# A recurrent attention block with a feed-forward block behind it: chunks of 32 problems on four quarters of the array, two scans for the decay, and a written-out order for all engines

## The chip, the cores and the metric

The kernel runs on one core of one Trainium2 chip. A core has five engines that work at the same time and wait for each other by semaphores: TensorE (PE, matrix products from SBUF into PSUM; its weight loads are listed apart as PEld), VectorE (DVE), ScalarE (ACT), GpSimd (POOL) and SyncE (SP), which here only issues DMAs. Each engine takes its instructions in program order. The metric is the device time in microseconds, so less is better. All data are 32-bit floats.

## The reference

For each of 4 batches and 8 heads there is one recurrence over 768 tokens with a 40x40 state; these 32 (batch, head) pairs are the "problems".

```python
for t in range(S):
    y[:, :, t] = np.einsum('bhd,bhde->bhe', rt, state)
    Sa = np.einsum('bhde,bhe->bhd', state, at)
    state_decay = state * wt[:, :, None, :] - np.einsum('bhd,bhe->bhde', Sa, bt)
    state = state_decay + np.einsum('bhd,bhe->bhde', vt, kt)
```

The output, turned to 3072 tokens by 320 channels, is then the input of a feed-forward block:

```python
h = x @ w_in                        # 320 -> 2048
g = h * (1.0 / (1.0 + np.exp(-h)))  # SiLU
return (g @ w_out).astype(np.float32)   # 2048 -> 320
```

The two weight matrices arrive as 64-bit floats; the kernel turns them into 32-bit floats on the chip by integer operations on their two words.

## The kernel before

Tokens are cut into 12 chunks of 64. A chunk has two units (`m` = 0, 1) of two batches, 16 problems each. Within a chunk the recurrence becomes matrix work. With W the running product of the decay w, a is multiplied by W, and b and k are divided by it (`scale`: a scan on VectorE at line 209, a reciprocal at 218, products on GpSimd at 219 and 221). `between` (line 189) makes the 64x64 products of b and a, and of k and a, between the tokens of the chunk, masked on VectorE at 197. One plus the masked b-a matrix has to be inverted: `inverse` does this for the two 32x32 halves of the matrices of two chunks at once (64 problem-chunks, 128 matrices, one on each partition) by 31 rows of a multiply (258) and a sum (264) on VectorE. The matrices go to it through DRAM (`md`, line 241) and come back through `xd` and `zd` (272 to 290). `merge` (302, 319) joins the halves with 32x32 products.

`chain` is the part that depends on the state: `keys` turns k and b (365), `right` makes the right-hand sides (374, 386), `solve` applies the inverse (408, 426), `update` makes the next state (446 on TensorE, 461 and 464 on VectorE, 470 on GpSimd), `turn` transposes it (477), `read` and `write` make the output (488, 496, 508, 515, 526). The output goes by 16 DMAs a chunk (line 532) from `yx` to `xt`, with channels on partitions. The feed-forward part `moe` takes `xt`: 16 groups of three products (549, rows 120, 120 and 80), a sigmoid on ScalarE (557) and a product on VectorE (558), then 2 x 16 products of the second layer (566), a copy (575) and the DMAs out (578). `weights` (lines 134 to 147) converts 44 pieces of the weight matrices.

What sets the order: the program text. `weave` mixes lists of steps evenly: the steps of the chains of chunk n, those that prepare chunk n+2 (and every second chunk the rows of the inverse), and what waits of the feed-forward part. Inputs are loaded on SP's queue two chunks ahead, weights on ScalarE's queue. `sb.tile` with `bufs` gives several buffers in turn; PSUM has six banks for the recurrence (`bank`) and two for the feed-forward part (`moe_bank`). If a running product leaves its range, a slow exact version behind `tc.If` runs instead; with these inputs it doesn't.

Of the kernel before, what the change touches and what calls it, by code (L numbers as in the profile page):

```python
# [18 lines left out]

TT = C = 64
DP = 64
# [4 lines left out]
def weave(*lists):  # L33

    at = [(i + 0.5) / len(x) for x in lists for i in range(len(x))]
    steps = [s for x in lists for s in x]
    for i in sorted(range(len(steps)), key=lambda i: at[i]):
        steps[i]()
# [3 lines left out]
def kernel(  # L42
# [16 lines left out]
    NM, NN = aT.shape[0] // 2, aT.shape[1]  # L59
    B, S = v.shape[0], v.shape[1]  # L60
    D, H, P, Q = 40, 8, 4, 8
    DM, DF = w_in.shape[0], w_in.shape[1] // 2
    NF = DF // 128
    KT = (120, 120, 80)
    assert (B, NM, NN * C, DM) == (4, 2, S, 320)
# [7 lines left out]
    def bank(name):  # L73
        return ps.tile([128, 512], F32, name=name, tag="att", bufs=6)

    def moe_bank(name):
        return ps.tile([128, 512], F32, name=name, tag="moe", bufs=2)

    ident = const.tile([128, 128], F32, name="ident")
    make_identity(nc, ident)  # L80
    ms = sb.tile([128, 2, C], F32, name="ms")
    ml = sb.tile([128, C], F32, name="ml")
    for be in range(2):
        make_upper_triangular(nc, ml[C * be : C * be + C], diag=False)
    nc.vector.tensor_copy(out=ms[:, 0], in_=ml)
    nc.vector.tensor_scalar(out=ms[:, 1], in0=ml, scalar1=-1.0, scalar2=None, op0=ALU.mult)
    wi_s = const.tile([128, 3, DF], F32, name="wi_s")
    wo_s = const.tile([128, NF, DM], F32, name="wo_s")
    chk = const.tile([128, 2 * NM * NN], F32, name="chk")

    one = sb.tile([128, Q, C + 1], F32, name="one")
    hm = sb.tile([128, 2], F32, name="hm")
    low = sb.tile([128, 1], F32, name="low")
    nc.vector.memset(low, -896.0 * 2.0**23)
    G = [sb.tile([128, Q, D], F32, name=f"G{m}") for m in range(NM)]
    Gbd = [sb.tile([128, Q, 2, DP], F32, name=f"Gbd{m}") for m in range(NM)]
    GT = [sb.tile([128, Q, 128], F32, name=f"GT{m}") for m in range(NM)]
    RHS = [sb.tile([128, P, 2, DP], F32, name=f"RHS{m}") for m in range(NM)]
    XT = [sb.tile([128, NM, H, C], F32, name=f"XT{i}") for i in range(2)]
    XI = sb.tile([128, 32, 32], F32, name="XI")  # L100

    w0 = sb.tile([128, Q, C + 1], F32, name="w")
    early = [
        sb.tile([128, 32 * 32], F32, name=x)[:, 0 : Q * (C + 1)].rearrange("p (q t) -> p q t", q=Q)
        for x in ("tmp", "mi")
    ]
    for w in [w0] + early:
        nc.vector.memset(w, 1.0)
        nc.vector.memset(w[:, :, 0:1], 0.0)
    nc.vector.memset(one, 0.0)  # L110
    nc.vector.memset(one[:, :, 0:1], 1.0)
    nc.vector.memset(hm, 0.0)
    for j in range(2):
        nc.vector.memset(hm[DP * j : DP * j + DP, j : j + 1], 1.0)
    nc.vector.memset(XI, 0.0)
    nc.vector.memset(XI.rearrange("p s t -> p (s t)")[:, 0 : 32 * 32 : 33], 1.0)
    for t in G + Gbd + GT + RHS + XT:
        nc.gpsimd.memset(t, 0.0)
# [4 lines left out]
    WS = 256  # L123
    pieces = [(wi_s[0:n, k, c : c + WS], w_in[120 * k : 120 * k + n, 2 * c : 2 * (c + WS)])
              for c in range(0, DF, WS) for k, n in enumerate(KT)]
    wo_f = wo_s.rearrange("p c d -> p (c d)")
    for c in range(0, NF * DM, WS):
        pieces.append((wo_f[:, c : c + WS], w_out[:, 2 * c : 2 * (c + WS)]))

    def weights(n):  # L130
        dst, src = pieces[n]
        m = dst.shape[0]
        room = sb.tile([128, 4 * WS], I32, name=("tmp", "mi")[n % 2])[0:m]
        nc.scalar.dma_start(room[:, 0 : 2 * WS], src)
        words = room[:, 0 : 2 * WS].rearrange("p (c two) -> p c two", two=2)
        lo, hi = words[:, :, 0], words[:, :, 1]
        e, f = room[:, 2 * WS : 3 * WS], room[:, 3 * WS : 4 * WS]
        shr, band, bor = ALU.logical_shift_right, ALU.bitwise_and, ALU.bitwise_or
        nc.vector.tensor_scalar(out=e, in0=hi, scalar1=20, scalar2=0x7FF, op0=shr, op1=band)  # L139
        nc.vector.tensor_scalar(out=f, in0=hi, scalar1=0xFFFFF, scalar2=None, op0=band)  # L140
        nc.scalar.activation(out=e, in_=e, func=AF.Relu, scale=2.0**23, bias=low[0:m])
        nc.scalar.activation(out=f.bitcast(F32), in_=f, func=AF.Copy, scale=2.0**-20, bias=1.0)
        nc.scalar.activation(out=lo.bitcast(F32), in_=lo.bitcast(U32), func=AF.Copy, scale=2.0**-52)
        nc.vector.scalar_tensor_tensor(out=e, in0=hi, scalar=-(1 << 31), in1=e, op0=band, op1=bor)
        f, lo, e = (x.bitcast(F32) for x in (f, lo, e))
        nc.vector.tensor_tensor(out=f, in0=f, in1=lo, op=ALU.add)
        nc.vector.tensor_tensor(out=dst, in0=f, in1=e, op=ALU.mult)  # L147

    class Unit:
        pass  # L150

    def unit(n, m):
        u = Unit()
        u.n, u.m, u.i = n, m, NM * (n % 2) + m
        return u


    def load(u):
        u.a = sb.tile([128, Q, C], F32, name="a", bufs=4)
        u.kb = sb.tile([128, Q, 2, C], F32, name="kb", bufs=6)  # L160
        B2 = slice(2 * u.m, 2 * u.m + 2)
        for n, x in ((1, bT), (0, kT)):
            for be in range(2):
                nc.sync.dma_start(
                    u.kb[:, P * be : P * be + P, n], x[2 * u.m + be, u.n].rearrange("p (q t) -> p q t", q=P)
                )
        nc.sync.dma_start(
            u.a.rearrange("p (b q) t -> p b (q t)", b=2), aT[B2, u.n].rearrange("b p c -> p b c")
        )

    def load_w(u, at):
        u.w = at
        for be in range(2):
            for j in range(2):
                J = slice(DP * j, DP * j + D)
                nc.sync.dma_start(
                    at[J, P * be : P * be + P, 1 : C + 1],
                    wT[2 * u.m + be, u.n, J].rearrange("p (q t) -> p q t", q=P),
                )

    def between(u, n, s):

        pm = [bank("pm") for _ in range(2)]
        for p in range(P):
            for be in range(2):
                for j in range(2):
                    q = P * be + p
                    J = slice(DP * j, DP * j + DP)
                    nc.tensor.matmul(  # L189
                        pm[j][C * be : C * be + C, p * C : p * C + C],  # L190
                        lhsT=u.kb[J, q, n, :],
                        rhs=u.a[J, q, :],
# [13 lines left out]
    def pre(u, md):  # L206
# [24 lines left out]
        def scores():  # L231
# [3 lines left out]
            if u.m < NM - 1:  # L235
                return
# [559 lines left out]
```

## Time and profile before

| | |
|---|---|
| Three runs | 1112.42 us median, 1108.23 to 1114.07 |
| Profiled execution | span 1101.0 us, from its first to its last instruction; no other time of this execution is given |
| TensorE, weight loads | 865.9 us (79%), 701.6 us (64%), 11058 instructions each |
| VectorE, ScalarE, GpSimd | 620.7 us (56%), 314.1 us (29%), 126.2 us (11%) |
| Mean granted clock of TensorE | 0.931 of full speed |
| DMA | 80.68 MB in 205707 packets, 73 GB/s; 176656 packets under 512 B |

A row of the page's list of groups reads: line, engine, operation, output<-inputs, shape, count, then busy time and mean duration, then the idle time of the engine before these instructions and what ended it. The rows with ten digits per engine cut the span into 40 slices of 27.5 us; a 9 is 90% busy or more, and PEclk is the granted clock in tenths. One f32 product appears as two MATMUL instructions. Matmuls overlap each other, so a mean duration of one (250 ns for a small one) is much longer than the distance between two.

### The profile page before, as it was taken

Reading aid. Unit: us, or ns where it says so; the run is one execution under the profiler, and the core shown is the slowest. Engines: PE = TensorE matmul, PEld = TensorE weight load, DVE = VectorE, ACT = ScalarE, POOL = GpSimd, SP = SyncE. Lnnn points to the kernel's source line nnn. Section 1 sums busy time; section 2 is a strip of 40 time slices with the busy share of each in tenths; the row PEclk is TensorE's granted clock in tenths of the full one; section 3 lists DMA queues with packets and bytes.
Section 4 is the critical chain, followed back from the end, with each engine's and each line's share of the span. In section 5 each row is a group of like instructions: output and inputs, shape, how many; then the busy total and the mean of one; then the engine's idle time right before and its main releaser. Section 6 shows DMA issues by size and latency. Waiting matters only on the chain.

```text
span 1101.0 us, 25962 instructions
## 1 busy us (share of the span) xinstructions
PE 865.9 (79%) x11058; PEld 701.6 (64%) x11058; DVE 620.7 (56%) x1088; ACT 314.1 (29%) x736; POOL 126.2 (11%) x136
## 2 busy tenths in 40 slices
PE   0003746777969999699998699987999997999997
PEld 0002745654648786478776578775787775887875
DVE  7497468886961469913559805479515597131220
ACT  2003536543214321124421233311342211432120
POOL 6100102300001120001110002200011200000000
PEclk9999977789987899889999799998898998999999
DMA  5604443543023351034341215431324213020000
GB/s 135 134 15 115 125 115 101 141 113 87 11 66 86 95 121 37 13 80 112 82 120 25 56 31 128 97 88 29 74 71 101 74 36 77 10 73 17 7 19 15
DMA packets 205707, 80.68 MB, mean 73 GB/s; under 512 B 176656, under 2 KB 198160, under 8 KB 205584
## 3 DMA queue, kind: packets, MB, share of 16 engines
q1 hardware_dynamic: 199776, 68.46, 26.2%
q10 hardware_dynamic: 5808, 10.49, 3.3%
q8 instruction: 88, 1.44, 0.5%
q14 instruction: 35, 0.29, 0.1%
HBM read 61.60 MB, written 13.37 MB: 68 GB/s over the span
## 4 chain that ended last, share of the span: by engine, by line
PE 44%; DVE 31%; DMA 9%; SPq 7%; issue 4%; POOL 2%; ACT 2%; DVEq 0%; ACTq 0%; POOLq 0%
PE ph L549 13%; DVE tmp L258 10%; PE po L566 10%; DVE XI L264 7%; SPq L532 4%; DVE w L218 4%; PE pl L488 3%; DVE gts L558 2%; PE pm L189 2%; PE pr L386 2%; PE pq L302 2%; DVE W L209 2%; DMA tmp<-in_w_in 2%; DMA xt<-yx 2%; PE pg L446 2%
## 5 line engine op out<-in xcount | busy, mean ns | idle before, releaser
L549 PE MATMUL ph<-xt,wi_s 120*128 120x256 f32 (+1 forms) x1152 | 296.9, 410 | 69.2 <-DVE gts L558 56.0
L549 PEld LDWEIGHTS ph<-xt,wi_s 120*128 120x128 f32 (+1 forms) x1152 | 225.0, 203 | 123.7 <-DVE gts L558 72.1
L566 PE MATMUL po<-wo_s,gts 128*128 128x320 f32 x768 | 222.6, 445 | 13.6 <-DVE wo_s L147 7.7
L566 PEld LDWEIGHTS po<-wo_s,gts 128*128 128x128 f32 x768 | 146.0, 194 | 74.4 <-DVE wo_s L147 9.4
L558 DVE TENSOR_TENSOR gts<-ph,sg 128x256 f32<-128x256 f32 x192 | 79.6, 418 | 147.0 <-ACT sg L557 146.4
L258 DVE TENSOR_TENSOR tmp<-XI,mi 128x1 f32<-128x1 f32 (+30 forms) x186 | 139.8, 752 | 15.6 <-DMA mi<-md 11.1
L557 ACT ACTIVATE sg<-ph 128x256 f32<-128x256 f32 x192 | 73.3, 383 | 253.5 <-PE ph L549 244.8
L264 DVE TENSOR_REDUCE XI<-tmp 128x1 f32<-128x1 f32 (+30 forms) x186 | 93.3, 502 | 5.0
L221 POOL TENSOR_TENSOR kb<-kb,w 128x512 f32<-128x512 f32 x44 | 53.6, 1239 | 362.5 <-DVE w L218 277.8
L197 DVE TENSOR_TENSOR sk<-pm,ms 128x256 f32<-128x256 f32 x48 | 18.2, 419 | 134.6 <-PE pm L189 134.6
L302 PE MATMUL pq<-XT,sb 32*32 32x32 f32 x768 | 33.0, 206 | 74.7 <-DMA XT<-zd 74.7
L189 PE MATMUL pm<-a,kb 64*64 64x64 f32 x1536 | 48.5, 251 | 52.3 <-POOL kb L221 41.8
L302 PEld LDWEIGHTS pq<-XT,sb 32*32 32x32 f32 x768 | 30.8, 122 | 81.9 <-DVE mi L139 61.9
L189 PEld LDWEIGHTS pm<-a,kb 64*64 64x64 f32 x1536 | 39.0, 156 | 63.0 <-POOL kb L221 44.8
L218 DVE RECIPROCAL w<-W 128x512 f32<-128x512 f32 x22 | 73.7, 3348 | 0.8
L219 POOL TENSOR_TENSOR a<-a,W 128x512 f32<-128x512 f32 x24 | 28.9, 1204 | 346.3 <-DMA a<-in_aT 242.7
L526 DVE TENSOR_TENSOR yx<-py,W 64x512 f32<-64x512 f32 x48 | 33.0, 688 | 37.8 <-DMA xt<-yx 14.0
L480 ACT COPY GT<-pt 128x512 f32<-128x512 f32 x44 | 24.2, 586 | 85.9 <-PE pt L477 85.7
L488 PE MATMUL pl<-r,vut 64*128 64x64 f32 x768 | 46.5, 274 | 0.0
L488 PEld LDWEIGHTS pl<-r,vut 64*128 64x128 f32 x768 | 44.2, 188 | 3.4 <-issue 3.0
L575 ACT COPY ot<-po 128x320 f32<-128x320 f32 x24 | 10.2, 425 | 114.9 <-PE po L566 92.0
L470 POOL TENSOR_TENSOR G<-t,W 128x320 f32<-128x320 f32 x22 | 25.4, 1156 | 130.4 <-DVE t L461 130.4
(101 smaller groups left out, 966.3 us busy)
## 6 DMA issues: line engine op xcount, KB each, us to landing
kb<-in_bT SPq DMA_DIRECT2D x48, 128.0 KB
kb<-in_kT SPq DMA_DIRECT2D x48, 128.0 KB
a<-in_aT SPq DMA_DIRECT2D x24, 256.0 KB
vut<-in_vT SPq DMA_DIRECT2D x48, 128.0 KB
r<-in_rT SPq DMA_DIRECT2D x24, 256.0 KB
v<-in_v SPq DMA_DIRECT2D x48, 80.0 KB
vu<-in_v SPq DMA_DIRECT2D x24, 160.0 KB
xt<-yx SPq DMA_DIRECT2D x192, 20.0 KB
```

The source lines that it names most:

```text
L189: nc.tensor.matmul(pm[j][C * be : C * be + C, p * C : p * C + C], lhsT=u.kb[J, q, n, :], rhs=u.a[J, q, :], start=True, stop=True,)
L218: nc.vector.reciprocal(R, u.W[:, :, 1 : C + 1])
L221: nc.gpsimd.tensor_tensor(out=u.kb[:, :, n], in0=u.kb[:, :, n], in1=R, op=ALU.mult)
L258: nc.vector.tensor_tensor(out=tmp[:, 0:t, 0:t], in0=XI[:, 0:t, 0:t], in1=mi[:, 0:t, t].unsqueeze(1).to_broadcast([128, t, t]), op=ALU.mult,)
L264: mark["row"] = nc.vector.tensor_reduce(out=XI[:, 0:t, t], in_=tmp[:, 0:t, 0:t], axis=AX.X, op=ALU.add).ins
L302: nc.tensor.matmul(pq[be][r + 32 : r + 64, h * 32 : h * 32 + 32], lhsT=s[r : r + 32, h, 32:64], rhs=X[r : r + 32, h, 32:64], start=True, s ...
L488: nc.tensor.matmul(pl[j][:, q * C : q * C + C], lhsT=u.vut[J, q].rearrange("p n t -> p (n t)"), rhs=u.r[J, q, :], start=True, stop=True,)
L532: nc.sync.dma_start(xt[r : r + D, h // 3, 2 * C * u.m : 2 * C * u.m + 2 * C].rearrange("e (b t) -> e b t", b=2), yx[DP * j : DP * j + D].r ...
L549: nc.tensor.matmul(ph[:, 0:T], lhsT=wi_s[0:rows, k, f * 128 : f * 128 + 128], rhs=xt[0:rows, k, :], start=k == 0, stop=k == 2,)
L557: nc.scalar.activation(out=sg, in_=ph[:, 0:T], func=AF.Sigmoid)
L558: nc.vector.tensor_tensor(out=gts[0][:, f, :], in0=ph[:, 0:T], in1=sg, op=ALU.mult)
L566: nc.tensor.matmul(po[m][:, 0:DM], lhsT=gts[0][:, f, m * 2 * C : m * 2 * C + 2 * C], rhs=wo_s[:, f, :], start=f == 0, stop=f == NF - 1,)
```

## The change

The recurrence and the feed-forward part are written anew; the mathematics, the inputs and the slow version are as before.

- A chunk is now one unit of all 32 problems. All small products take 40 or 64 rows and 40 or 64 columns of the array, in one of its four quarters; the loops run so that the quarters take turns. Turning k, b and the state is done by such products with a piece of the identity, in place of 128x128 transposes.
- Decay: the scan now runs backwards over the chunk with a reset in every problem, and gives V, by which b and k are multiplied; a second, forward scan on the decay, started from the reciprocal of the chunk's total, gives Z, by which a and the output are multiplied. The state is kept in the scale of the chunk's end and multiplied by `wc`. The reciprocal is taken of 16 numbers instead of 512.
- The inverse runs over rows from the last to the first, and reads its matrix along the row.
- The output takes the way through DRAM (`xh`): two DMAs there and three back. The feed-forward input is cut into 128, 128 and 64 rows; the 64-row products (`rest`, line 975) of two column groups lie in the two row halves. SiLU is one ScalarE instruction for 1024 elements.
- Weights are converted in 20 pieces of 512 columns, in places that are not in use yet.
- All work is entered in a list with an engine, an assumed cost, what it reads and writes, a priority, and the PSUM pair (two banks, four pairs in all) or buffer that it needs. `Plan.order` then simulates the engines with these costs and fixes the order in which every engine issues. The feed-forward products have the lowest priority, so they fill gaps on TensorE; they may hold two pairs, the next state one.

The core of the diff; lines with "..." leave out code.

```diff
-def weave(*lists):
+class Plan:
+    def add(self, engine, cost, do, r=(), w=(), pri=0, rooms=(), mode="", size=0.0, after=0.0):
...
+    HOP = {"SP": 0.1, "ACT": 0.15, "PE": 0.12, "DVE": 0.12, "POOL": 0.2}
+    SLACK = {"SP": 0.0, "ACT": 0.1, "PE": 0.4, "DVE": 0.15, "POOL": 0.1}
+    SWITCH = 0.2
+    def order(self):
...
+        while len(out) < len(ops):
+            best = None
+            for e, some in ready.items():
+                starts = []
+                for op in some:
+                    s = max(at[e], op["ready"])
...
+                    if e == "PE" and op["mode"] != mode:
+                        s += self.SWITCH
+                    starts.append((s, op))
...
+                least = min(s for s, _ in starts)
+                s, op = min(((s, op) for s, op in starts if s <= least + self.SLACK[e]), key=lambda x: (x[1]["pri"], x[1]["n"]))
...
+            if op["size"]:
+                dma[e] = max(dma[e], end) + op["size"] / 150.0
+                end = dma[e] + 2.0
...
+    def dma(do, size, r=(), w=(), pri=0, engine="SP", rooms=()):
+        add(engine, 0.06, do, r, w, pri, rooms, size=size)
...
-            nc.vector.reciprocal(R, u.W[:, :, 1 : C + 1])
+        def scans():
+            nc.vector.memset(vf[:, F : F + 1], 1.0)
+            nc.vector.tensor_tensor_scan(back(vf[:, 0:F]), back(wf), back(zf), 1.0, ALU.mult, ALU.add)
+        def scan2():
+            nc.vector.tensor_tensor_scan(wf, wf, zf, 0.0, ALU.mult, ALU.add)
+        add("DVE", 2.4, scans, [*allw, "zt"], vkey, pri)
+        add("DVE", 0.15, lambda: nc.vector.reciprocal(zt[:, :, 0], Wc), vkey, ["zt"], pri)
+        add("DVE", 2.3, scan2, ["zt"], allw, pri)
...
+        def between(name, room):
+            slots = (1, 2) if name == "b" else (0, 3)
+            for o in problems("m", "z", "x", "b", "j"):
+                b, j, x, m, z = (o[k] for k in "bjxmz")
+                g = 4 * m + 2 * z + x
+                nc.tensor.matmul(
+                    room.tile[half(b), j, g * C : g * C + C],
+                    lhsT=kbv[rows(j), slots[b], m, 2 * z + x, :],
+                    rhs=A[rows(j), 8 * b + 4 * m + 2 * z + x, :],
...
+        add("PE", 1.0, partial(between, "b", pb_), keys["b"] + akeys, [pb_, ("sb", i2)], pri, [pb_], "q")
...
+            def row(s=s, m_=m_):
+                nc.vector.tensor_tensor(
+                    out=tmp[:, 0:m_, 0:m_],
+                    in0=XI[:, s + 1 :, s + 1 :],
+                    in1=mi[:, s, s + 1 :].unsqueeze(1).to_broadcast([128, m_, m_]),
+                    op=ALU.mult,
+                )
+                nc.vector.tensor_reduce(out=XI[:, s + 1 :, s], in_=tmp[:, 0:m_, 0:m_], axis=AX.X, op=ALU.add)
...
+        def rest(g0):
+            for g in (g0, g0 + 1):
+                for f in (0, 2, 1, 3):
+                    h = f // 2
+                    nc.tensor.matmul(
+                        rooms[g].tile[:, h, (f % 2) * T : (f % 2) * T + T],
+                        lhsT=wi3[half(h), g * 256 + (f % 2) * 128 : g * 256 + (f % 2) * 128 + 128],
+                        rhs=xt[half(h), 2],
...
+        def gate(g):
+            nc.scalar.activation(
+                out=gts[:, 4 * g * T : 4 * g * T + 4 * T], in_=rooms[g].tile.rearrange("p a b -> p (a b)"), func=AF.Silu
+            )
...
+            add("PE", 3.5, partial(full, g), [("xt", 0), *w_(g)], [a_, ("gts", g), ("gts", g + 1)], pri + g, [a_], "f")
+            add("PE", 1.8, partial(rest, g), [("xt", 1), ("xt", 2), ("wi3", g // 2)], [a_, b_], pri + g + 0.1, [a_, b_], "h")
...
+    for n in range(NN):
+        merge(n)
+        chain(n)
+        read(n)
+        moe(n)
...
+    with tc.manual_schedule():
+        for op in plan.order():
+            op["do"]()
```

In the new kernel the lines that matter are: scans 432 and 435, scalings on GpSimd 452 and 459, `between` 470, the mask 502, k-a times values 517, turning k and b 541, rows of the inverse 571 and 577, matrices to DRAM 489 and back 566 to 611, merge 625 and 654, `right` 696, `values` 720, `solve` 737 and 749, turning the state 790, `update` 817 with 832 and 841 on VectorE, `look` 866 with its mask 878, `write` 897 (state) and 910 (128 rows), output scaling 924, to DRAM 939 and back 953 and 955, feed-forward 962, 975 and 985, second layer 1001, copy 1013 and out 1016, weights 304 to 324.

## The prediction

> **What bounds the kernel now.** I read four views in this order: the page (shares, slices, costliest groups), the table of stages, the timeline of TensorE, and the chain that ended last. The page first:
>
> ```profile
> span 1101.0 us, 25962 instructions
> PE 865.9 (79%) x11058; PEld 701.6 (64%) x11058; DVE 620.7 (56%) x1088; ACT 314.1 (29%) x736; POOL 126.2 (11%) x136
> PE   0003746777969999699998699987999997999997
> DVE  7497468886961469913559805479515597131220
> PEclk9999977789987899889999799998898998999999
> L549 PE MATMUL ph<-xt,wi_s 120*128 120x256 f32 (+1 forms) x1152 | 296.9, 410 | 69.2 <-DVE gts L558 56.0
> L566 PE MATMUL po<-wo_s,gts 128*128 128x320 f32 x768 | 222.6, 445 | 13.6 <-DVE wo_s L147 7.7
> L258 DVE TENSOR_TENSOR tmp<-XI,mi 128x1 f32<-128x1 f32 (+30 forms) x186 | 139.8, 752 | 15.6 <-DMA mi<-md 11.1
> L218 DVE RECIPROCAL w<-W 128x512 f32<-128x512 f32 x22 | 73.7, 3348 | 0.8
> ```
>
> No average says it: the slices do. TensorE does nothing for the first three slices (82 us), is half starved up to the thirteenth, and is nearly full afterwards, while VectorE is densest at the start. The stages, cut where the first feed-forward product runs (161.9), where starvation ends, and where the recurrence ends:
>
> ```profile
> 0.00:161.90 161.90, 44.67 (x993) 41.28 (x993) 107.72 (x202) 42.35 (x98) 30.16 (x41) 0.96 0.45 107
> 161.90:350.00 188.10, 144.06 (x1443) 112.61 (x1443) 134.58 (x264) 74.00 (x177) 20.22 (x18) 0.82 0.32 83
> 350.00:950.00 600.00, 534.38 (x6999) 432.58 (x6995) 347.82 (x560) 162.51 (x378) 73.04 (x76) 0.94 0.31 74
> 950.00:1101.00 151.00, 142.84 (x1634) 115.09 (x1632) 30.62 (x63) 35.22 (x84) 2.75 (x2) 0.98 0.10 24
> ```
>
> Columns are stretch, length, then busy us of PE, PE's weight loads, DVE, ACT and POOL, the granted clock, DMA share and GB/s. So there are three limits: VectorE and loads until about 350 us, with TensorE at a clock of 0.82 [...]; TensorE with 11% idle to 950; TensorE alone at the end. The timeline gives prices at full clock, from one row's start to the next's (rows overlap at their ends):
>
> ```profile
> 660.41 0.69 PE L189 MATMUL pm<-a,kb 64*64 64x64 f32 x32
> 661.04 0.77 PE L374 MATMUL pr<-Gbd,a 128*64 128x80 f32 x16
> ...
> 671.11 3.79 PE L488 MATMUL pl<-r,vut 64*128 64x64 f32 x64
> 674.83 1.15 PE L508 MATMUL py<-r,GT 64*64 64x64 f32 x32
> 675.91 1.15 PE L515 MATMUL py<-lam,kt 128*64 128x64 f32 x32
> 676.99 1.15 PE L508 MATMUL py<-r,GT 64*64 64x64 f32 x32
> ```
>
> Every f32 product is two instructions. Spread over four quarters (L189) one costs 0.63/32 = 19.7 ns; on two diagonal quarters (L508) 34 ns; with 128 rows and half the columns (L515) 34; with 64 rows and all columns (L488) 58. In the same view 64 of the 32x32 ones take 1.24 us, 19.4 each, and the 128x128 turns 118. The end of the chain that ended last prices the feed-forward part:
>
> ```profile
> 1037.44 17.23 PE po L566 x64
> 1056.55 19.76 PE ph L549 x90
> ```
>
> That is 269 ns and 219 ns.
>
> [...] six L566 between two 32x32 groups take 1.81 us instead of 1.61, so 0.2 for a change from wide to narrow. [...]
>
> **The change, part by part.** TensorE: at these prices the old program is 306 us of small products plus 1152 x 0.219 = 252 plus 768 x 0.269 = 207, 765 in all, against 866 busy: the rest is clock (0.93) and changes of mode. The new order has 5184 quarter products (x2 x 19.7 ns = 204), 768 of 32x32 (30), 384 with 128 rows (26), 384 full first-layer products (168), 384 second-layer ones (207), and 192 half-height ones of L975 in two row halves. The last are not in the old trace: at best two run together, 384 x 109 ns = 42; at worst 84. I take 42, since quarters do overlap. Sum 677, 88 less than 765.
>
> VectorE: out go 24 reciprocals (80 us), the SiLU products (80; ScalarE does SiLU in 48 instructions of about 1.03 us, from 0.383 for 256 elements and 0.59 for 512, against 73 for the sigmoids), and the doubled state (Gbd, 20). In come 24 scans of 1040 elements at 2.4 (old 1.24 for 520) = 58 against 30, and some copies from PSUM (24 of about 0.6). Masks and outputs halve in number and double in width, which saves only the fixed 0.16 us. Weights: 20 pieces of five operations, about 2.9 us each (1.83 for 256 elements, doubled, less five fixed costs), 58 instead of about 90. The inverse reads its matrix without the 32-word step. Its multiply costs 23.3 us per inverse and its reduce 15.5 for as many elements; I let it gain 0 to 8, and take 5. VectorE comes to about 445 instead of 621, under TensorE: it matters at the start only. POOL does as many elements as before in the scalings and less otherwise; with 126 us before it is covered by TensorE.
>
> Start: SP now issues 68 DMAs (60 loads, 8 for r and v) ahead of the eight that write the matrices. Its rows show 0.57 to 0.65 us each, so those eight end at about 2 + 68 x 0.6 + 8 x 0.5 = 47, and the inverse, 8.6 us after the last group's first issue in the old trace (39.69 to 48.27), begins near 56 instead of 48. Ahead of it VectorE has two chunks' scans and four weight pieces, which fit. The rows take 40 us now, about 35 then: 91, against 88.5. From there twelve weight pieces stand before chunk 0's output on VectorE: 35 us by VectorE, 47 by 6.3 MB at the 134 GB/s of the first slices; I take 39, plus 8 for its own work: 138. The output then goes through DRAM (two trips of about 2 us, five issues): 145, where the old kernel has 162. All TensorE work behind it in the order waits for that.
>
> Rest: 33 us of TensorE work come before, so 644 remain. The order holds 169 changes of tiling, about 40 of them wide to narrow: 15 us with some for the rest. At a clock of 0.97, between the 0.94 and 1.00 of dense stretches, (644 + 15)/0.97 = 679. Idle: while a pair of chunks runs its chain (merge, solve, update, next state, twice) hardly any feed-forward product lies between; the chain's own waits for copies then show. I take 7%, 48 us, less than the 11% of the middle stage because the list puts feed-forward groups where the planner saw a wait. The end, from last product to last instruction, was 7.5: 7. Sum 145 + 679 + 48 + 7 = 879 of span. The profiled execution's span of 1101.0 is 11 under the median 1112.42; the same 11 gives 890.
>
> The new SP order holds about 118 issues for a pair of chunks, 71 us at 0.6, inside the 125 us of TensorE work for a pair; without that cover each late matrix DMA holds the chain. SP is strictly in order: out, loads for the chunk after next, and the matrix traffic queue behind one another, and the feed-forward input of the next chunk behind all of these. The planner prices an issue at 0.06, so its order sees none of that. ScalarE, about 190 us plus SiLU, remains idle most of the time.
>
> **Rivals.**
> 1. The likeliest: as summed, 835 to 935. The margin holds the L975 case (+43), 15 us at the start, and the idle share from 3 to 12%.
> 2. Quarters run at the diagonals' 34 ns: 10368 x 14 ns / 0.97 = +150, so 1040. For it: weights of 40 columns and other orders of quarters than L189's; L426, also four quarters, looks like 25. Against: 19.4 on 32x32.
> 3. The fixed order does not fit the chip and TensorE gets no better yield than before: the work after 161.9 was about 730 us at full clock in 939, 0.78. Then 145 + 644/0.78 + 7 + 11 = 989. Four PSUM pairs, of which the feed-forward part may hold two and the state one, speak for it.
> 4. Quicker: the planner's own 1.0 us for 32 quarter products (mine 1.26), less idle: below 830.
> 5. Slower than before: the inverse loop becomes the bound. There is one mi, XI, tmp and kb. Per pair, in series: matrix writes and read 8.6, rows 35 with up to 30 of other VectorE work between, back copy and reload 9.5 (88.5 to the first pq at 98.1), merges 5, two chains 20: about 108, hidden by 125 of TensorE work. To end at 1112 each of five pairs has to take 125 + 222/5 = 169, so each loop would have to lose 61 us to SP's queue. SP waited 119 us for ScalarE's output copies in all in the old run, 30.5 the longest.
>
> **The numbers.** Chances: case 1 0.62, 2 0.11, 3 0.14, 4 0.05, 5 0.07, no change 0.01. Predicted 890. The range 820 to 995 holds cases 1 and 3 and half of 4; the likeliest one's own is 835 to 935. A difference of 0.5% is about what a measurement of this kernel can tell: faster 0.92, within it 0.01, slower 0.07.
>
> **What would show it.** First L962 near 145 and no long wait after it; L470, L541 and L866 at about 1.26 us for a group of 64 instructions; L975 near 109 ns apart; TensorE over 92% busy from 200 us; VectorE near 445 us. Wrong if L470 groups take 2 us, if TensorE waits tens of microseconds for X or ZQ in every pair, or if xt lands late because SP stood before another wait.

## The result, and the profile after

The changed kernel takes 950.1 us (median; 943.2 to 951.5) where the kernel before took 1111.2 us beside it: a ratio of 0.853, 95% interval 0.850 to 0.857. That is inside the range given, 60 us above its point, and above the 835 to 935 of its likeliest case. The profiled execution took 951.08 us and has a span of 949.2 us.

First the page of the kernel after, the same rows as before: shares, slices of 23.7 us, costliest groups, and the row of the DMA queue that carries instructions (packets, MB, share of the engines).

```profile
span 949.2 us, 31784 instructions
PE 739.9 (78%) x14594; PEld 602.9 (64%) x14594; DVE 447.7 (47%) x690; ACT 197.6 (21%) x254; POOL 103.2 (11%) x85
PE   0430152898978898988889889799789989999997
DVE  6459779632952348823479135594354932000000
PEclk9999996868996779996989867899779999999999
q8 instruction: 116, 1.90, 0.9%
L1001 PE MATMUL pair<-wo,gts 128*128 128x320 f32 x768 | 230.3, 458 | 8.1 <-DVE ot L1013 7.6
L962 PE MATMUL pair<-xt,wi 128*128 128x256 f32 x768 | 186.4, 401 | 6.4 <-DMA xt<-xh 6.4
L571 DVE TENSOR_TENSOR tmp<-XI,mi 128x1 f32<-128x1 f32 (+30 forms) x186 | 100.6, 541 | 23.4 <-DMA mi<-md 17.4
```

VectorE is where it was expected, 447.7 us. TensorE's busy time fell from 866 to 740, but its share of the span did not rise: 78%, where it was 79%. And the clock row, which before dipped to 7 and 8, now has sixes and sevens far into the kernel. The stages, with the columns of the table before (stretch, length, busy us of PE, its weight loads, DVE, ACT and POOL, clock, DMA share, GB/s), cut at the first feed-forward product:

```profile
0.00:166.80 166.80, 44.33 (x1537) 41.85 (x1537) 117.27 (x187) 45.29 (x64) 29.34 (x31) 0.95 0.55 132
166.80:300.00 133.20, 117.10 (x2380) 95.01 (x2381) 68.57 (x112) 36.08 (x47) 15.75 (x12) 0.85 0.29 71
300.00:800.00 500.00, 437.91 (x9998) 359.32 (x9999) 256.62 (x383) 99.83 (x127) 58.09 (x42) 0.85 0.30 76
800.00:949.20 149.20, 140.60 (x688) 106.73 (x682) 5.21 (x10) 16.38 (x16) 0.00 (x0) 0.99 0.08 20
```

The long middle stage is 88% busy at a clock of 0.85. Before, it was 89% busy at 0.94. What that looks like in one pair of chunks, in TensorE's timeline (start, length, group, and in brackets the idle time before it with what ended it):

```profile
420.09 0.38 PE L625 MATMUL pair<-ZQ,sb 32*32 32x32 f32 x21
422.68 0.57 PE L625 MATMUL pair<-ZQ,sb 32*32 32x32 f32 x43 [2.21 <-issue]
423.18 2.23 PE L866 MATMUL pair<-r,vut 40*64 40x64 f32 x85
426.40 1.55 PE L866 MATMUL pair<-r,vut 40*64 40x64 f32 x43 [0.99 <-issue]
427.88 1.92 PE L654 MATMUL pair<-X,ZQ 32*32 32x32 f32 x64
429.72 1.95 PE L696 MATMUL pair<-G,a 40*64 40x40 f32 x64
...
437.71 1.14 PE L737 MATMUL pair<-extra,X 64*64 64x40 f32 x64
...
439.72 0.42 PE L817 MATMUL pair<-u,kt 64*40 64x40 f32 x20
441.45 0.62 PE L817 MATMUL pair<-u,kt 64*40 64x40 f32 x43 [1.31 <-issue]
```

Three things are to be seen. Groups of 64 take either about 1.1 us or about 1.9, at full and at half clock (granted 1.00 from 437.70 to 440.00, 0.50 from 425.00 to 431.60). The pauses stand in the middle of a group (21 + 43, 20 + 43), so a copy or a buffer for the group is hardly what is waited for, and the profile names nothing: "issue". And they come at a fixed count: 85 + 43 = 128 pairs of weight load and product from one to the next. Over the same stretch the instruction queue moves packets of 16 KB (they start at 419.94, 423.73, 427.50, 431.01 and 434.46, and TensorE resumes at 422.68 and 426.40, 2.7 us after the first two); 1.90 MB in 116 packets, and 116 times 128 covers the 14594 pairs. In all, "issue" takes 46.2 us in 38 pauses after 150 us; before it took 2.6 us in 5.

The start, on SyncE's queue:

```profile
20.34 16.07 SPq L355 DMA_DIRECT2D wz<-in_wT  x16
...
47.91 6.70 SPq L489 DMA_DIRECT2D md<-sb  x8
...
151.78 0.76 SPq L939 DMA_DIRECT2D xh<-lam  x2
152.58 11.30 SPq L355 DMA_DIRECT2D wz<-in_wT  x16
163.92 0.44 SPq L953 DMA_DIRECT2D xt<-xh  x1
```

Sixteen loads for a later chunk are issued between the writing of the first output to DRAM and its reading back; the first L962 starts at 166.76.

### The profile page after: what moved, and what is told of

The parts are those of the page before. It is cut to its first block, busy times and chain, and to the rows that moved or that the text cites. A ratio compares the mean times of both kernels' runs of the same rounds, so it can differ in the third digit from the quotient of the medians.

```text
span 949.2 us, 31784 instructions
## 1 busy us (share of the span) xinstructions
PE 739.9 (78%) x14594; PEld 602.9 (64%) x14594; DVE 447.7 (47%) x690; ACT 197.6 (21%) x254; POOL 103.2 (11%) x85
## 5 line engine op out<-in xcount | busy, mean ns | idle before, releaser
L1001 PE MATMUL pair<-wo,gts 128*128 128x320 f32 x768 | 230.3, 458 | 8.1 <-DVE ot L1013 7.6
L1001 PEld LDWEIGHTS pair<-wo,gts 128*128 128x128 f32 x768 | 151.7, 201 | 74.3 <-DVE ot L1013 11.6
L962 PE MATMUL pair<-xt,wi 128*128 128x256 f32 x768 | 186.4, 401 | 6.4 <-DMA xt<-xh 6.4
L962 PEld LDWEIGHTS pair<-xt,wi 128*128 128x128 f32 x768 | 152.3, 201 | 35.6 <-DMA xt<-xh 6.5
L571 DVE TENSOR_TENSOR tmp<-XI,mi 128x1 f32<-128x1 f32 (+30 forms) x186 | 100.6, 541 | 23.4 <-DMA mi<-md 17.4
L985 ACT ACTIVATE gts<-pair 128x1024 f32<-128x1024 f32 x48 | 49.1, 1023 | 246.7 <-PE pair L975 144.1
L452 POOL TENSOR_TENSOR kb<-kb,vd 128x512 f32<-128x512 f32 x44 | 65.1, 1506 | 127.0 <-DVE vd L432 28.8
L625 PE MATMUL pair<-ZQ,sb 32*32 32x32 f32 x768 | 11.1, 203 | 60.6 <-DMA ZQ<-zd 52.4
L866 PE MATMUL pair<-r,vut 40*64 40x64 f32 x1536 | 41.7, 276 | 13.9 <-issue 12.8
L975 PE MATMUL pair<-xt,wi 64*128 64x256 f32 x384 | 52.0, 414 | 0.0
L625 PEld LDWEIGHTS pair<-ZQ,sb 32*32 32x32 f32 x768 | 9.1, 114 | 63.8 <-issue 61.8
L866 PEld LDWEIGHTS pair<-r,vut 40*64 40x64 f32 x1536 | 37.6, 185 | 17.9 <-issue 16.0
L975 PEld LDWEIGHTS pair<-xt,wi 64*128 64x128 f32 x384 | 37.6, 200 | 10.4 <-issue 6.0
L910 PE MATMUL pair<-lam,kt 128*40 128x64 f32 x768 | 33.5, 266 | 7.8 <-DVE lam L878 7.8
L910 PEld LDWEIGHTS pair<-lam,kt 128*40 128x40 f32 x768 | 31.4, 153 | 9.3 <-DVE lam L878 7.9
```

What stands on the lines that cost most here:

```text
L452: TTn[engine].tensor_tensor(out=x[:, b], in0=x[:, b], in1=y[:, b], op=ALU.mult)
L571: nc.vector.tensor_tensor(out=tmp[:, 0:m_, 0:m_], in0=XI[:, s + 1 :, s + 1 :], in1=mi[:, s, s + 1 :].unsqueeze(1).to_broadcast([128, m_, m_]),
L625: nc.tensor.matmul(p1.tile[64 * x + 32 : 64 * x + 64, b, c * 32 : c * 32 + 32], lhsT=S_[64 * b : 64 * b + 32, g, 32:64], rhs=ZQ[64 * b : 6 ...
L866: nc.tensor.matmul(pl.tile[half(1 - b if role else b), b, c * C : c * C + C], lhsT=vut[rows(b), role, hh, :], rhs=rs[rows(b), hh, :], star ...
L910: nc.tensor.matmul(py.tile[rows(j), b, c * C : c * C + C], lhsT=K[:, j, q, :], rhs=lam[m].tile[:, l * C : l * C + C], start=(b, j) not in ...
L962: nc.tensor.matmul(rooms[g].tile[:, f // 2, (f % 2) * T : (f % 2) * T + T], lhsT=wi[:, k, (4 * g + f) * 128 : (4 * g + f) * 128 + 128], rh ...
```

## Experiments

The theories. **F**: TensorE's instructions arrive in blocks of 16 KB, 128 pairs, at best one in about 3.45 us; quarter products use a block in 2.1 us, so a long run of them starves, and the pauses bring the clock down. **G**: the clock falls by itself, because quarters count for little. **H**: the pauses are waits for copies and PSUM pairs. **S**: SyncE's order and the number of its issues set the start and hold later chunks. All edits are to the changed kernel; all but the first two programs do the whole computation.

**Instruction blocks by themselves.** A separate program with none of the kernel's computation: stretches of small products between stretches of full ones.

```diff
+        quarters(768)
+        wide(64)
+        quarters(256, n=256)
+        wide(64)
+        for _ in range(24):
+            quarters(32)
+            wide(8)
+        wide(64)
+        tall(768)
+        wide(64)
+        quarters(768, rows=64)
+        wide(64)
...
+        for k in range(16):
+            nc.sync.dma_start(bg[:, 1024 * (k % 4) : 1024 * (k % 4) + 1024], x[:, 1024 * (k % 6) : 1024 * (k % 6) + 1024])
+        quarters(768)
```

`quarters` has weights of 40 x 64 and 64 columns if nothing else is said, `tall` 128 x 64 and 64 columns, `wide` 128 x 128 and 256 columns.

> A program of its own, nothing of the computation in it: stretches of quarter products (weights 40 x 64, 64 columns) set apart by stretches of 64 full products (128 x 128, 256 columns); no copies, no DMA. Three theories. F: TensorE's instructions arrive in blocks of 16 KB (128 weight-load and matmul pairs), at best one in 3.5 us, so a quarter product that needs 16 ns per instruction takes 27 in a long run, and the clock falls only because of the pauses. G: the clock falls by itself, because 40 rows of a quarter do not count as work for the throttle; no pauses. H: neither; the pauses in the changed kernel are waits for copies and PSUM. First stretch, 768 products (1536 pairs): F 41 us, a pause of about 1.4 us after every 128th pair, half clock from somewhere in it; G 25 to 46 us, half clock, no pauses; H 25 us. Second, 256 products of 256 columns (512 pairs, an estimated 55 to 66 ns each): F no pauses, full clock, 28 to 34 us; G half clock, about double. Third, 24 times 32 quarter products (64 pairs) and 8 full ones (16): F no pauses, full clock, 24 x (1.05 + 3.5 + 0.2) = 114 us; G clock partly down. Fourth, 768 products of 128 rows by 64 columns at 30.5 ns: F 47 us, next to no pauses, 128 take 3.9 us. Fifth, as the first with 64 rows: F as the first; G better clock. Sixth, as the first with 8 MB of loads under way: F longer than the first, blocks come over the same DMA engines; G and H as the first.

The six stretches in the table of stretches, in this order, with the columns of the table of stages; then TensorE's timeline of the fifth:

```profile
34.27:77.37 43.10, 38.95 (x1537) 37.27 (x1536) 0.00 (x0) 0.00 (x0) 0.00 (x0) 0.60 0.02 4
106.60:134.40 27.80, 27.80 (x513) 19.49 (x512) 0.00 (x0) 0.00 (x0) 0.00 (x0) 1.00 0.01 2
162.20:272.40 110.20, 110.20 (x1905) 92.63 (x1904) 0.00 (x0) 0.00 (x0) 0.00 (x0) 1.00 0.01 2
303.70:348.70 45.00, 45.00 (x1538) 44.93 (x1537) 0.00 (x0) 0.00 (x0) 0.00 (x0) 1.00 0.02 4
376.50:417.60 41.10, 24.95 (x1537) 23.45 (x1536) 0.00 (x0) 0.00 (x0) 0.00 (x0) 1.00 0.02 4
452.80:503.20 50.40, 41.61 (x1537) 39.86 (x1536) 0.00 (x0) 0.00 (x0) 0.00 (x0) 0.56 0.35 129
```

```profile
384.78 2.09 PE L26 MATMUL pr<-a 64*64 64x64 f32 x128 [1.36 <-issue]
388.23 2.09 PE L26 MATMUL pr<-a 64*64 64x64 f32 x128 [1.36 <-issue]
391.69 2.09 PE L26 MATMUL pr<-a 64*64 64x64 f32 x128 [1.36 <-issue]
```

With no copies and no waits at all, 128 pairs take 2.09 us (16.3 ns each) and then TensorE stands for 1.36 us: a block in 3.45. Stretches whose 128 pairs need longer than that (256 columns, 7.0 us; 128 rows, 3.75; a mixture with full products, 7.4) have no such pauses, and loads in the background lengthen the first stretch from 43 to 50 us. In the fifth stretch, every pause shown ends 2.3 to 2.4 us after an instruction packet of 16 KB starts (382.48, 385.83 and 389.28). So F's blocks are shown, and H is not needed for the pauses. On the clock neither F nor G had it whole: with the same pauses, 40-row quarters fell to half clock (0.60 over the stretch) and 64-row ones did not (1.00), while 40-row quarters without pauses kept full clock (1.00 in the second stretch).

**The clock, and how much mixing is enough.**

```diff
+        quarters(512, n=128)
+        quarters(768, rows=64, n=32, cols=40)
+        for k in (64, 96, 128):
+            for _ in range(12):
+                quarters(k)
+                wide(8)
...
```

> A second program of its own, nothing of the computation in it, again stretches set apart by 64 full products. First, 512 quarter products of 40 rows and 128 columns (1024 pairs, about 27 to 30 ns each, so 128 take about one block's 3.45 us): if the clock falls for pauses together with few rows, full clock and next to no pauses; if 40 rows alone lower it, half clock. Second, 768 products of 64 rows, 40 weight columns and 32 columns: 1.3 to 1.5 us of work per 128 pairs, so a pause of about 2 us after each, period 3.45 again, 41 us in all; if rows times busy time counts, half clock here at 40% busy with 64 rows. Third, fourth and fifth, 12 times 128, 192 and 256 pairs followed by 16 full pairs: 2.1, 3.1 and 4.2 us of small products and 3.5 of full ones, 5.9, 7.0 and 8.0 us with the change of tiling, against 3.9, 5.6 and 7.3 us for the instruction blocks: no pauses, or short ones in the fifth, and full clock. So up to 192 pairs between groups of full products can be fed. Sixth and seventh, 64 rows and 40 rows as in the first program: 41 us at full clock with a pause of 1.36 us per block, and half clock from about 8 us on.

The first five stretches, same columns:

```profile
33.80:62.30 28.50, 28.49 (x1026) 28.00 (x1025) 0.00 (x0) 0.00 (x0) 0.00 (x0) 1.00 0.02 5
90.10:132.70 42.60, 25.64 (x1537) 24.19 (x1536) 0.00 (x0) 0.00 (x0) 0.00 (x0) 0.57 0.02 4
162.70:227.20 64.50, 64.50 (x1713) 56.02 (x1712) 0.00 (x0) 0.00 (x0) 0.00 (x0) 1.00 0.01 3
258.50:340.80 82.30, 76.76 (x2481) 67.57 (x2481) 0.00 (x0) 0.00 (x0) 0.00 (x0) 1.00 0.02 4
372.10:482.70 110.60, 97.78 (x3249) 85.28 (x3248) 0.00 (x0) 0.00 (x0) 0.00 (x0) 0.92 0.02 4
```

40 rows without pauses: full clock (1.00), so G falls. 64 rows with 1.4 us of work in a block of 3.45: half clock (0.57 over the stretch; these products also have 40 weight columns instead of 64). The last two stretches repeated the first program, 64 rows at 1.00 and 40 rows at 0.55. So in these stretches the clock fell only where there were pauses, and for 40 rows at a busy share at which 64 rows kept it. Rows times busy share at full clock (2.09 or 1.43 us of the 3.45) puts the four cases in order: 40 x 1.00 = 40 and 64 x 0.61 = 39 kept it, 64 x 0.41 = 26 and 40 x 0.61 = 24 did not. That is a fit to four points, one of which has other columns as well, and not a rule. In the clock records of the changed kernel the granted clock is 1.00 or 0.50, and every stretch at 0.50 lasts a multiple of 3.41 us (3.41 to 20.48), but for the last one, 5.42 us up to the end of the records. In the stretches of the two programs without loads the longest pause was 2.03 us. With 128 pairs between full products nothing pauses; with 192, where none were expected, there are pauses of 0.95 to 1.37 us in five of twelve rounds; with 256 in eleven, and the clock dips to 0.92 on average.

**SyncE's order alone.** The decay loads between `xh` (at `j`) and each `xt` load (at `i`) go behind the latter, unless something in between needs them; no other engine's order changes.

```diff
-        for op in plan.order():
+        order = plan.order()
...
+            span = order[j + 1 : i + 1]
+            late = [op for op in span if op.get("tag") == "wz" and not any(op["n"] in x["before"] for x in span)]
+            order[j + 1 : i + 1] = [op for op in span if op not in late] + late
+        for op in order:
             op["do"]()
```

> The changed kernel with one edit in SyncE's order: the up to 16 loads of the decay factors of a later chunk, which stand between the writing of a chunk's output to DRAM and the loads that read it back as the feed-forward input, are issued after those loads. Theory S (the late start is SyncE's order): the first L962 comes at 157 instead of 166.8, and the time falls by 7 to 12 us, to about 940. Rival: the feed-forward products were waiting for something else by then, weights or PSUM, or what starts earlier is lost again within the next chunks because TensorE's order is fixed: within 0.3% of the changed kernel.

963.3 us, ratio 0.864 (0.858 to 0.870): slower than the changed kernel, not faster. The first L962 did start at 156.9, 9.8 us earlier, and half-way TensorE was 17 us behind the changed kernel, with the same sequence of products. It lost 10 us between 338 and 359 and 14 us between 407 and 496. Two of its waits, over the whole run (us in all, times, the longest), and two instructions of VectorE:

```profile
PE pair L471 <- POOL wz L937: 9.0, 1, 9.0
PE pair L911 <- DVE lam L879: 17.2, 2, 9.4
335.29 2.33 DVE L433 TENSOR_TENSOR_SCAN vd<-wz,zt 128x1040 f32<-128x1040 f32 x1 [10.47 <-DMA wz<-in_wT]
472.14 2.33 DVE L433 TENSOR_TENSOR_SCAN vd<-wz,zt 128x1040 f32<-128x1040 f32 x1 [15.30 <-DMA wz<-in_wT]
```

The first ends at 344, the longest of the second at 476, so both lie where the time was lost; in the changed kernel there is no wait for the first, and one of 7.8 us for the second. Ahead of both, VectorE's scan of the decay waited for the loads that had been moved back, 10.5 and 15.3 us. The products of a and b need what the scan makes; the mask `lam` does not, but it comes behind the scan in VectorE's program order. So S in the form "the order is wrong" falls: with 16 issues per chunk, either the feed-forward input or the scan came late in the two orders tried.

**TensorE's order.** The planner takes a feed-forward group first after every small group, or after every two (`key` stands at the end of its line).

```diff
-    key=lambda x: (x[1]["pri"], x[1]["n"])
+    key=lambda x: (e == "PE" and small >= 1 and x[1]["mode"] not in ("f", "h"), x[1]["pri"], x[1]["n"])
...
             if e == "PE":
                 mode = op["mode"]
+                small = 0 if mode in ("f", "h") else small + 1
```

> The changed kernel with one edit in the planner: on TensorE, after every group of the recurrence (32 products, 64 pairs) a group of the feed-forward part is taken first if one can start within the planner's slack. The long runs of small products, 12 to 24 us in the plan, are broken up except where PSUM leaves no place. By the planner's own clock this is worse: 801 us instead of 751. F (instruction blocks): pauses put down to issue fall from 46 us to under 15, half clock from 192 us to under 110, 65 more changes from wide to narrow cost 13 us, so about 890 to 915. H (the pauses are waits for copies and PSUM, which the planner knows): slower, 965 to 1000.

> The same with two groups of the recurrence (128 pairs, one block of instructions) between feed-forward groups: the planner's own clock says 764 instead of 751. F: between the two, pauses of issue about 20 us, half clock 100 to 140 us, 42 more changes of tiling (8 us): about 900 to 925. H: 955 to 970.

After every group (threshold 1): 962.8 us, 0.862 (0.857 to 0.867). Half clock after the first L962 fell from 189 to 156 us and "issue" from 46 to 26, but idle time in all rose from 87 to 122: the recurrence is held up, as H and the planner had it, and F's 890 to 915 failed. After every two (threshold 2): 928.9 us, 0.831 (0.827 to 0.835). "Issue" fell to 8.5 us and half clock to 132, and the other waits grew from 41 to 85 us (`ot` from 7.6 to 25.0, `lam` of line 502 from 8.1 to 14.0). F said 900 to 925, H 955 to 970; F's mechanism holds and its gain was partly eaten. The traces show some of what ate it: VectorE's scans waited 81 us for the decay loads here, against 31 in the changed kernel, and one such wait of 16.9 us (until 580.0) comes just ahead of a wait of TensorE of 5.9 us (until 584.4). The longest wait, 11.9 us for the output copy `ot`, had another cause: on VectorE the copy stood behind rows of the inverse.

**Fewer issues on SyncE.** Eight decay loads of 40 rows per chunk.

```diff
-    for part in (slice(64 * j, 64 * j + 32), slice(64 * j + 32, 64 * j + D)):
+    for part in (slice(64 * j, 64 * j + D),):
```

> The changed kernel with the decay factors of a chunk loaded by 8 DMAs of 40 rows instead of 16 of 32 and 8 rows: 96 issues fewer on SyncE, at 0.7 to 1.0 us each 67 to 96 us of its time, 16 or so of them at the start ahead of the matrices and 8 ahead of the first feed-forward input. Theory S (SyncE's issues are a bound of their own, at the start and before later chunks): first L962 at about 145 to 152 instead of 166.8, and the time 915 to 935. Rival (the start is lost again as in the kernel with the loads moved): 945 to 955.

917.9 us, 0.826 (0.819 to 0.833). The time is as S had it. The first L962 starts at 139.1, 28 us earlier and earlier than expected, which is nearly all of the gain; "issue" is 53 us and half clock 169. SyncE spent 77 us on the 96 loads, 0.81 each, against 129 on 192, 0.67 each, so 51 us were saved and not the 67 to 96 expected.

**Together.** Price means the planner's cost of an issue on SyncE (`add(engine, 0.06, ...)` in `dma`).

> Three edits at once: 8 decay loads per chunk, the planner's price of an issue on SyncE 0.5 instead of 0.06 us, and a feed-forward group preferred on TensorE after every three groups of the recurrence (192 pairs). If instruction blocks and SyncE each cost what the single edits showed and they add up: pauses of issue under 15 us, half clock under 110 us, first L962 before 155, and about 880 to 905. If they overlap, no better than the single ones, 925.

> The same with a feed-forward group after every two groups of the recurrence. If instruction blocks are what matters, two and three differ by the changes of tiling alone, so 0 to 8 us above the kernel with three; if the clock needs the full products closer together, below it.

> The kernel with a feed-forward group after every two of the recurrence and 8 decay loads, but with the planner's price of an issue on SyncE back at 0.06 us. The two edits alone gave about 25 us (order of TensorE) and 30 us (8 loads), the three together 92. If order and loads help each other (a chain that gets its loads in time can use the better order), this is 857 to 872 and the price little; if the price made the difference, 890 to 900, the plain sum.

> 8 decay loads and a price of 0.5 us for an issue on SyncE, TensorE's order left to the planner as in the changed kernel. If instruction blocks and the clock are the larger part of what is lost, this stays near the kernel with 8 loads: 905 to 925, half clock above 150 us, and the order of TensorE is then worth 50 to 65 us against the kernel with all three edits. If SyncE is the larger part: 870 to 890.

Ratio to the kernel before, and TensorE's idle time and the time at half clock, from the first L962 to the last product (the 192 us of the expectations count to the end of the span):

| kernel | median us | ratio (interval) | first L962 | idle us | half clock us |
|---|---|---|---|---|---|
| changed kernel | 950.1 | 0.853 (0.850-0.857) | 166.8 | 87 | 189 |
| every 2 | 928.9 | 0.831 (0.827-0.835) | 165.6 | 94 | 132 |
| 8 loads | 917.9 | 0.826 (0.819-0.833) | 139.1 | 89 | 169 |
| 8 loads, price 0.5 | 936.8 | 0.842 (0.837-0.847) | 154.1 | 92 | 183 |
| 8 loads, every 2 | 851.4 | 0.764 (0.761-0.768) | 139.4 | 59 | 88 |
| 8 loads, every 2, price 0.5 | 857.1 | 0.770 (0.765-0.776) | 153.3 | 61 | 68 |
| 8 loads, every 3, price 0.5 | 876.2 | 0.785 (0.778-0.791) | 151.5 | 73 | 82 |

The two edits give 25 and 30 us alone (0.022 and 0.027 of 1112) and 99 together. With 8 loads the order takes away 81 us of half clock and 30 of idle time; with 16 it took 57 and none. The scans' wait for the decay loads, 81 us with 16 loads and every two, is 21 with 8 loads and every two, which fits the thought that late loads ate the gain of the order. But a rival stays: whatever is changed in the planner's list or costs, it writes a new order for all engines. With 8 loads alone, the kind of product differs at 3854 of 14594 places on TensorE, with the price on top of it at 10284. So each row of the table belongs to one whole order, and no run separates the edit from luck in the order that it led to.

The price with 8 loads came out at 936.8, above both of its expectations; it brings the first L962 15 us later. At a price of 0.5, every two is better than every three, the case set down for "the clock needs the full products closer together". It has less half clock, but also 6 us of "issue" against 30 (under 15 were expected with three), so clock and blocks are not told apart here. A piece of the recurrence's chain in the kernel with 8 loads and every two:

```profile
401.97 0.83 PE L722 MATMUL pair<-extra,kt 64*40 64x40 f32 x64
402.75 1.14 PE L739 MATMUL pair<-extra,X 64*64 64x40 f32 x64
403.82 2.42 PE L1003 MATMUL pair<-wo,gts 128*128 128x320 f32 x8
406.17 0.83 PE L819 MATMUL pair<-u,kt 64*40 64x40 f32 x64
406.81 1.09 PE L751 MATMUL pair<-X,extra 64*40 64x64 f32 x64
407.83 2.42 PE L1003 MATMUL pair<-wo,gts 128*128 128x320 f32 x8
```

No pause, and every group in the time of full clock (L722 in 0.83 us, L739 in 1.14; L737 of the changed kernel took 1.14 at a granted 1.00).

**A better version.** The copy of the feed-forward output moved from VectorE to ScalarE, with a price of 0.7, and then the copy alone.

```diff
-    add(engine, 0.06, do, r, w, pri, rooms, size=size)
+    add(engine, 0.06 if engine == "ACT" else 0.7, do, r, w, pri, rooms, size=size)
-    add("DVE", vec(320), lambda b=b: nc.vector.tensor_copy(out=ot[0], in_=po.tile[:, b, 0:DM]), [(po, b)], ["ot"], 10 * n, [po])
+    add("ACT", act(320), lambda b=b: nc.scalar.copy(out=ot[0], in_=po.tile[:, b, 0:DM]), [(po, b)], ["ot"], 10 * n, [po])
```

> All three edits with a price of 0.7 us, what the issues of these loads take in the traces, and the output of the feed-forward part copied from PSUM by ScalarE instead of VectorE, behind which TensorE's second-layer products waited 34 us in the kernel with all three edits. If that wait is real and ScalarE, busy for 23% of the span, takes the copy at once: 825 to 845. Rival: the wait goes over to ScalarE, behind the copies of the recurrence, and the time stays at 850 to 860.

> A feed-forward group after every two of the recurrence, 8 decay loads, the output of the feed-forward part copied by ScalarE, and the planner's price of an issue on SyncE at 0.06 us as in the changed kernel: one edit (the copy) against the kernel with order and loads alone (851.4), and one (the price of 0.7) against the best so far (832.8). If the 20 us that TensorE waits there for VectorE's copy of the output are what the best one saved: 833 to 842. If the price did it: 848 to 855.

Both: 832.8 us, 0.748 (0.744 to 0.752), the fastest, below both kernels, with 39 us idle and 58 at half clock. The copy alone: 848.7 us, 0.763 (0.758 to 0.768), no different from 0.764. TensorE's waits in the kernel with 8 loads and every two, then with the copy moved as well (edits shift the line numbers a little: L1003 is L1001 of the changed kernel, L519 is L517):

```profile
PE pair L1003 <- DVE ot L1015: 20.3, 5, 11.2
PE pair L519 <- DVE lam L504: 6.1, 1, 6.1
```

```profile
PE pair L519 <- DVE lam L504: 19.0, 2, 11.5
PE pair L1003 <- ACT ot L1015: 2.1, 4, 0.6
```

The wait for `ot` went from 20.3 to 2.1 us, and one for `lam` grew by 13: it was only moved on. The longest of each (11.2 us until 352.7, 11.5 until 361.4) ends behind rows of the inverse, which VectorE runs in front of the copy or the mask. What the best version gained came with the price of 0.7, alone or with the copy, and with the order that it led to; 0.7 without the copy was not run (0.5 without it gave 0.770).

## Why the prediction was right and where it was wrong

The direction and most of the size were right, but the likeliest case was too quick, and the total is as near as it is because the products were priced too high, which hid a third of the misses. Its sum against the trace of the changed kernel (the products counted, each at the mean distance that its line shows at full clock: 768 L962 at 221 ns, 767 L1001 at 272, 384 L975 at 120, and 11136 small ones at 16.4 on average, 182 us; the clock is what remains):

| term | predicted us | measured us |
|---|---|---|
| up to the first L962 | 145 | 166.8 |
| products after it, at full clock | 644 | 607 |
| clock and changes of tiling | 35 | 82 |
| TensorE idle | 48 | 87 |
| end | 7 | 6 |
| span | 879 | 949 |

Start, clock and idle time came out 22, 47 and 39 us above it and the products 37 below: 70 us in the span. Ten of these come back in the median, which lies 0.9 us above the profiled span and not the 11 taken over from before. Those 11 were no overhead: the executions listed with their spans in these runs take 1.7 to 1.9 us more than the span, so the profiled execution of before was most likely a quicker one than the three timed.

**Yield: the step that failed.** "At a clock of 0.97, between the 0.94 and 1.00 of dense stretches" and "I take 7%, 48 us ... because the list puts feed-forward groups where the planner saw a wait". The planner sees no wait where instructions are late, so it puts nothing there: runs of 12 to 24 us of small products in its plan, 46 us of pauses, and half clock for 189 us. The clock of dense stretches was taken over from a kernel in which more than half of the small products (about 5300 of 9138 instructions) took 28 ns or more each, above the 27 at which blocks arrive. The trace of before had a faint sign, 12 intervals under 4 us between instruction blocks after 150 us against 42 now, but only 2.6 us of pauses. Cheaper products, 10 to 18 ns at full clock, made it a limit. Rival 3's yield of 0.78 came out exactly, 607/(949.2 - 166.8 - 6.3) = 0.78, but not for its reason: with the same four PSUM pairs, another order and fewer loads raised it to 0.86 (607/(849.3 - 139.4 - 6.3)). Of the signs that it named, TensorE was 89% busy from 200 us and not over 92%, and the groups of 64 took 1.1 us at full clock and 1.9 at half, not 1.26.

**Prices.** 19.7 ns for a quarter product was too much: at full clock it is 10 to 12 ns where the weights and the input both have 40 columns, and 15 to 18 where either has 64. Of the two 32x32 groups one takes 10.7 (L625) and one 17.6 (L654). The 34 ns rival is out. The bounded term, L975, came to 120 ns against 109 taken and 219 at worst; L962 221 and L1001 272 as priced, L910 30.5 against 34.

**Start.** The terms: writes of `md` ended at 54.6 (47 predicted), because the 32 decay loads took 27.2 us (0.7 us each, then 1.0) and not 0.6 each, and the eight writes 6.7 us and not 4, while the other loads were mostly cheaper than 0.6 (0.42 to 0.46); from there to the first row 14.9 us instead of 9; rows 33.5 us (35); from the last row to the output 48.8 (47); and from the output to the first L962 15.0 instead of 7. The last is the place that the prediction named, "the feed-forward input of the next chunk queues behind all of these", "its order sees none of that", and then costed as five issues. Sixteen loads stood in between. So `xt` did land late, one of the prediction's signs of being wrong, though SyncE was busy issuing and did not stand before another wait.

**VectorE** at 447.7 us and the rows of the inverse were as summed. Rival 5, the inverse loop, did not come: of 52.4 us that TensorE waited for `ZQ`, 51.6 are the first pair's.

## What to carry to other kernels

When products get short, price the instructions too: find the rate at which blocks of them arrive (here at best 128 pairs in 3.45 us at a regular pace), and let the order put longer products between short ones before a run outlasts a block. Two edits may give more together than the sum of both, here 25 and 30 us alone and 99 together; but where a list scheduler sets the order, every edit of its input is also another order, so compare several before a gain is put down to one of them. A late load can hold up work that doesn't need it: here VectorE's scan waited 15.3 us for one, and TensorE 9.4 us for the mask that came behind the scan. A pause in the middle of a group, with no releaser and at a fixed count (here 1.36 us after every 128 pairs in a program without copies), pointed to the supply of instructions rather than to a dependency; a program with nothing else in it can show which.

## What was not expected of the hardware

- 128 pairs of weight load and product are one block of 16 KB (1.90 MB in 116 packets for 14594 pairs, and pauses 128 pairs apart); the shortest regular period is 3.45 us, whatever the product (2.09 or 1.43 us of work in it), and 5.1 and 6.5 us between the first blocks under 8 MB of loads. So in the long runs here a pair came to 27 ns or more (3.45 us for 128), though it needs 10 to 18. After a stretch of full products 159 to 224 pairs ran before the first pause.
- The clock went to half with 40-row quarters at 60% busy (0.60 and 0.55 over the stretches), kept full with 64-row ones at the same share (1.00), went to half with 64-row ones of 40 weight columns at 41% (0.57), and kept full for 40 rows without pauses (1.00).
- The 32- or 8-row decay loads took SyncE 0.7 to 1.0 us each in the bursts of 16 at the start (0.67 on average over the run), most of the 48-row loads beside them 0.42 to 0.46. The 40-row loads in their place took 0.81 on average, so halving the number saved 40% of the time.
